# Moving the last set's output weights behind the last rows of V in a decode-attention kernel

## The chip, the cores and the metric

The kernel runs on one core of one Trainium2 chip. The metric is the device time of one execution in microseconds (us), as the median of three runs.

## The reference, cut to what matters

One token attends to two caches, A with 16 heads and B with 16 query heads on 8 key/value heads, each with 8192 positions of 256 numbers. Each result goes through an output matrix `wo`, and a gate mixes the two rows of 448 numbers.

```python
def _A_ref(x, k_cache, v_cache, wq, wo):
    ...
    scores = jnp.einsum("bhqd,bhkd->bhqk", q, k_cache) * (Dh ** -0.5)
    p = _softmax(scores, axis=-1)
    o = jnp.einsum("bhqk,bhkd->bhqd", p, v_cache)
    return (lambda x, *d: x.transpose(*d))(o, 0, 2, 1, 3).reshape(B, Sq, H * Dh) @ wo
...
g = _sigmoid((x * gate_w).sum(-1, keepdims=True))
a = _A_ref(x, A_k_cache, A_v_cache, A_wq, A_wo)
b = _B_ref(x, B_k_cache, B_v_cache, B_wq, B_wo)
return g * a + (1 - g) * b
```

## The kernel before, in words

The work is cut into eight sets. A set holds one key/value head of B with its two query heads (unit 2) and two heads of A (units 0 and 1), and the units are done in the order 2, 0, 1 (`UNITS`). Everything is 32-bit. A unit's K and V come from memory in 4 MB transfers, two per unit for K and two for V, into a ring of five slots of 4 MB (`slot`). One loop runs over the transfers: at step i it issues K of step i and V of step i-1, then computes `scores` for step i (K times the query, exponentials, a transpose into `pr`), then `attend` for step i-1 (V times `pr`, summed in PSUM in the tile `o`). All of these loads are issued by SP, in program order, into one queue that the chip's 16 DMA engines work off; an issue waits until its slot has been read and until an earlier landing has freed the semaphore it counts on.

When a unit is done, `combine` and `column` work out the softmax weights of its rows on small tiles, `take` reads `o` into `ob`, `project_o` multiplies `ob` by the column of weights (`sel`) and copies the result to `ocs`, and `emit` multiplies `ocs` by the unit's part of `wo` and adds to `Y`, which stays in PSUM for the whole kernel. A set's `wo` is four heads of [128 rows, 896 numbers], 3,584 bytes a row and head; a 128-row head has 448 KB.

The last step (i = N) has no K. Before the change SP issues there, in this order: `wo` of heads 2 and 3, `wo` of head 0, the last V in pieces of 16, 8, 4 and 4 rows (`LAST_CUT`), and `wo` of head 1, the one that the last unit needs. TensorE (PE) does `combine` and `column` of the last unit, then `emit` of units 2 and 0 of the last set, then `attend` of the last V piece by piece, then `project_o` and `emit` of unit 1. For this last unit alone, `take(last=True)` copies the two halves of `o` unscaled, and `project_o` uses four products with two half columns (`selh`) in place of two.

Of the kernel before, what the change touches and what calls it, by code (L numbers as in the profile page):

```python
# [7 lines left out]
F32 = mybir.dt.float32  # L8
BF16 = mybir.dt.bfloat16
AF = mybir.ActivationFunctionType  # L10
OP = mybir.AluOpType
# [3 lines left out]
P = 128  # L15
D = 448
DH = 256
# [7 lines left out]
NS = 8  # L25
# [8 lines left out]
WQ = (2 * KF + 1) * DH  # L34
UNITS = [2, 0, 1]
LAST_CUT = [16, 8, 4, 4]


@with_exitstack
def kernel(  # L40
# [12 lines left out]
    nc = tc.nc  # L53
    scale = DH ** -0.5
# [3 lines left out]
    small = ctx.enter_context(tc.tile_pool(name="small", bufs=2))  # L58
# [7 lines left out]
    def heads(u):  # L66
        return 2 if u[1] == 2 else 1
# [42 lines left out]
    half = const.tile([P, 2], F32, name="half")  # L110
# [26 lines left out]
    def prepare():  # L137
        clear(Y, YN)
        gp = ps_s.tile([1, 1], F32, name="sm")
        for c in range(KF + 1):  # L140
            nc.tensor.matmul(gp, xs[:, c:c + 1], gw[:, c:c + 1], start=(c == 0), stop=(c == KF))
        ge = const.tile([1, 1], F32, name="ge")
        nc.scalar.activation(ge, gp, AF.Exp, scale=-1.0)
        nc.vector.tensor_scalar(ge, ge, 1.0, None, op0=OP.add)
        nc.vector.reciprocal(gate[:, 0:1], ge)
        nc.vector.tensor_scalar(gate[:, 1:2], gate[:, 0:1], -1.0, 1.0, op0=OP.mult, op1=OP.add)

    KT, VT, ST, PR, O, GS, SEL, OB, OC = ({} for _ in range(9))

    def project(u, w):  # L150

        s, r = u
        M = heads(u)
        q = ps_s.tile([P, 2, 2], F32, name="sm")
        n = 2 * DH
        for m in range(M):
            h = m if r == 2 else r
            for e in range(2):
                for c in range(KF):
                    at = c * n + h * DH + e * P  # L160
                    nc.tensor.matmul(q[:, e, m:m + 1], w[:, at:at + P], xs[:, c:c + 1], start=(c == 0), stop=False)  # L161
                at = KF * n + e * P
                nc.tensor.matmul(q[:, e, m:m + 1], w[:, at:at + P], xs[:, KF + h:KF + h + 1], start=False, stop=True)  # L163
        qb = QB[s % 2, r]
        nc.vector.tensor_scalar(qb[:, :, 16:16 + M], q[:, :, :M], -scale, None, op0=OP.mult)  # L165
# [34 lines left out]
            nc.tensor.matmul(O[u, part][32 * g:32 * (g + 1), :], pr[:, j // 2, :2 * NG * R], vt[:, j - j0:j - j0 + 2, :],  # L200
                             start=False, stop=(tt == R // M - 1 and j >= NB - 2 * NG), skip_group_check=True)

    def take(u, t, last=False):

        M = heads(u)
        part, tt = divmod(t, R // M)
        if tt != R // M - 1:
            return
        o = O.pop((u, part))
        ob1 = small.tile([P, DH], F32, name="ob1", bufs=1)  # L210
        ob = small.tile([P, DH], F32, name="ob", bufs=3)
        if last:
            nc.scalar.activation(ob1, o[:, DH:], AF.Copy)
            nc.vector.tensor_copy(ob, o[:, :DH])
            OB[u] = [(ob, SELH[0]), (ob1, SELH[1])]
        else:
            nc.scalar.activation(ob1, o[:, DH:], AF.Copy, scale=half[:, 1:2])  # L217
            nc.vector.scalar_tensor_tensor(ob, o[:, :DH], half[:, 0:1], ob1, op0=OP.mult, op1=OP.add)  # L218
            OB.setdefault(u, []).append((ob, None))

    def gather(u):
        M = heads(u)
# [34 lines left out]
                    ew[:, m, a * (n // M):(a + 1) * (n // M)][:, None, :, None].to_broadcast([1, NG, n // M, 2]),  # L257
                    rz[:, m:m + 1], None, op0=OP.mult)

    SELH = []  # L260

    def column(u, last=False):
        M = heads(u)
        cl = ps_s.tile([P, 2, 2], F32, name="sm")
        for a in range(M):
            for m in range(M):
                nc.tensor.matmul(cl[:, a, m:m + 1], WR[M][:, m, a].rearrange("p c x k -> p (c x k)"), one,  # L267
                                 start=True, stop=True)
        SEL[u] = small.tile([P, 2, 2], F32, name="sel")
        if last:  # L270
            for k in range(2):
                SELH.append(small.tile([P, 1], F32, name=f"selh{k}"))
                nc.vector.tensor_scalar(SELH[k], cl[:, 0, :1], half[:, k:k + 1], None, op0=OP.mult)
        else:
            nc.vector.tensor_copy(SEL[u][:, :M, :M], cl[:, :M, :M])

    def project_o(u):
        M = heads(u)
        oc = ps_s.tile([P, 2, 2], F32, name="sm")
        terms = [(ob, sel if sel is not None else SEL[u][:, a, :M]) for a, (ob, sel) in enumerate(OB[u])]  # L280
        for e in range(2):
            for k, (ob, sel) in enumerate(terms):
                nc.tensor.matmul(oc[:, e, :M], ob[:, e::2], sel, start=(k == 0), stop=(k == len(terms) - 1))  # L283
        ocs = small.tile([P, 2, 2], F32, name="ocs", bufs=4)
        nc.vector.tensor_copy(ocs[:, :, :M], oc[:, :, :M])  # L285
        OC[u] = ocs

    def emit(u, wt, last=False):
        for m in range(heads(u)):
            h = u[1] + m  # L290
            for e in range(2):
                for g in range(NG):
                    nc.tensor.matmul(Y[32 * g:32 * g + 1, :], OC[u][:, e, m:m + 1],  # L293
                                     wt[:, h, e, g * YN:(g + 1) * YN], start=False,
                                     stop=(last and m == heads(u) - 1 and e == 1), skip_group_check=True)


    work = [((s, r), t) for s in range(NS) for r in UNITS for t in range(0, NT, TL)]
    N = len(work)
    PER = len(UNITS) * NT // TL  # L300
    W, WO = {}, {}

    def load_wq(s):
        w = const.tile([P, 2 * WQ], F32, name="wq", bufs=1)
        nc.sync.dma_start(w, wq[s])
        for pair in range(2):
            W[s, pair] = w[:, pair * WQ:(pair + 1) * WQ]

    def load_k(i):
        u, t = work[i]  # L310
        kt = slot([TL, 2, NG, NB * BLK])
        nc.sync.dma_start(kt, of(u, a_k, b_k)[t // TL])
        KT[i] = kt
# [5 lines left out]
    def load_v(i, j0, n):  # L319
        vt = slot([n, DH])  # L320
        nc.sync.dma_start(vt, v_src(i)[:, j0:j0 + n, :])
        for k in range(0, n, ROWS):
            VT.setdefault(i, []).append((j0 + k, min(n, ROWS), vt[:, k:min(n, k + ROWS)]))

    def load_wo(s, parts):
        if s not in WO:
            WO[s] = const.tile([P, 4, 2, D], F32, name="wo", bufs=1)
        for h0, h1 in parts:
            nc.sync.dma_start(WO[s][:, h0:h1], wo[s][:, h0:h1])
# [3 lines left out]
    for i in range(N + 1):  # L333
        s = i // PER
        if i == 0:
            load_wq(0)
        if i < N:
            load_k(i)
        if i % PER == 2 and s + 1 < NS:
            load_wq(s + 1)  # L340
        if 0 < i < N:
            load_v(i - 1, 0, TL * ROWS)
        if i % PER == 0 and 0 < i < N:
            load_wo(s - 1, [(0, 4)])
        if i == N:
            load_wo(NS - 1, [(2, 4), (0, 1)])
            j0 = 0
            for n in LAST_CUT:
                load_v(N - 1, j0, n)
                j0 += n  # L350
            load_wo(NS - 1, [(1, 2)])


        if i == 0:
            for r in UNITS:
                project((0, r), W[0, 1 if r == 2 else 0])
            prepare()
        if i < N:
            u, t = work[i]
            kt = KT.pop(i)  # L360
            for k in range(TL):
                scores(u, t + k, kt[:, k])
            if t + TL == NT:
                gather(u)
                if i < N - 1:
                    COMB[i + 1] = u
        if i in COMB:
            combine(COMB[i])
        if i == N:
            u = work[N - 1][0]  # L370
            combine(u)
            column(u, last=True)
            emit((u[0], 2), WO[u[0]])
            emit((u[0], 0), WO[u[0]])
        if i > 0:
            u, t = work[i - 1]
            for j0, n, vt in VT.pop(i - 1):
                k, j = divmod(j0, ROWS)
                attend(u, t + k, j, n, vt)
                if j + n == ROWS:  # L380
                    take(u, t + k, last=(i == N))
        if i in COMB:
            column(COMB[i])
        if i - 1 in COMB:
            u = COMB[i - 1]
            project_o(u)
            if u[1] == UNITS[-1]:
                for r in UNITS:
                    emit((u[0], r), WO[u[0]])
        if s + 1 < NS and i % PER in (3, 4, 5):  # L390
            r = UNITS[i % PER - 3]
            project((s + 1, r), W[s + 1, 1 if r == 2 else 0])
    s = NS - 1
    project_o((s, 1))
    emit((s, 1), WO[s], last=True)

    ys = const.tile([P, YN], F32, name="ys")
    nc.vector.tensor_copy(ys, Y)
# [59 lines left out]
```

## Time and profile before

| | |
|---|---|
| median of 3 runs | 1021.46 us (1021.17 to 1021.71) |
| the profiled execution | 1021.16 us, its span in the profile 1019.3 us |
| PE busy | 660.9 us (65% of the span) |
| DVE busy, ACT busy | 209.2 us (21%), 98.9 us (10%) |
| moved by DMA | 432.68 MB, mean 425 GB/s |

The span runs from the first to the last recorded instruction; the execution's own time is 1.9 us longer. Times in the profile's views count from the span's start. PEld is PE's weight load, which overlaps its matmuls. A 32-bit matmul appears as two records, so `x28` is 14 matmuls. A share of DMA is the mean over 16 engines: 0.50 can be eight busy engines.

### The profile page before, as it was taken

To read this page: it belongs to the slowest core of one execution; us is meant where nothing else is said; L and a number is where in the kernel's file an instruction comes from. 1 tells how busy PE (TensorE), PEld (TensorE's weight loads), DVE (VectorE), ACT (ScalarE), POOL (GpSimd) and SP (SyncE) were. 2 spreads that over 40 slices of the span, in tenths; PEclk is the share of its full clock that TensorE was granted. 3 is DMA by queue.
4 is the path that set the end of the run, shared out by engine and by line. 5 is a ranking of instruction groups with operands and counts; after the bars stand their busy time and mean duration, and the time that the engine had idled before them with its cause. 6 is when DMAs were issued, how large, how long until landed. Compare 5 with 4: busy or idle time off the path is not lost.

```text
span 1019.3 us, 10424 instructions
## 1 busy us (share of the span) xinstructions
PE 660.9 (65%) x4493; PEld 250.1 (25%) x4493; DVE 209.2 (21%) x650; ACT 98.9 (10%) x258; POOL 0.6 (0%) x6
## 2 busy tenths in 40 slices
PE   6666757477575765749656487455875557746765
PEld 5113212133121321214212133121421214212212
DVE  1222212212122121222112221222212222121221
ACT  0101001000011000110001000010001100001000
POOL 0000000000000000000000000000000000000000
PEclk9768867786677887777667776787867878777668
DMA  9999999999999999999999999999999999999995
GB/s 394 424 430 431 430 436 427 431 430 432 429 431 431 428 431 430 432 430 430 428 430 429 431 430 431 432 426 431 431 430 434 429 430 428 429 432 431 431 426 241
DMA packets 17189, 432.68 MB, mean 425 GB/s; under 512 B 2168, under 2 KB 2168, under 8 KB 2808
## 3 DMA queue, kind: packets, MB, share of 16 engines
q1 hardware_dynamic: 16856, 432.02, 98.8%
q8 instruction: 35, 0.57, 0.2%
q14 instruction: 10, 0.08, 0.0%
q10 hardware_dynamic: 288, 0.00, 0.0%
HBM read 432.02 MB, written 0.00 MB: 424 GB/s over the span
## 4 chain that ended last, share of the span: by engine, by line
DMA 79%; PE 15%; another core or an unknown queue 4%; DVE 1%; issue 0%; ACT 0%; DVEq 0%; ACTq 0%
DMA slot<-in_a_v_dram 32%; DMA slot<-in_a_k_dram 32%; DMA slot<-in_b_k_dram 9%; PE sc L176 7%; PE o L200 6%; DMA slot<-in_b_v_dram 5%; PE sm L161 1%; DMA wq<-in_wq_dram 1%; PE sm L267 0%; PE sm L163 0%; DVE pr L187 0%; ACT ew L246 0%; PE o L133 0%; PE sm L283 0%
## 5 line engine op out<-in xcount | busy, mean ns | idle before, releaser
L200 PE MATMUL o<-slot,pr 128*32 128x512 f32 x1536 | 263.5, 846 | 205.3 <-DMA slot<-in_a_v_dram 112.4
L176 PE MATMUL sc<-slot,qb 128*32 128x512 f32 x1536 | 270.4, 868 | 127.2 <-DMA slot<-in_b_k_dram 65.9
L200 PEld LDWEIGHTS o<-slot,pr 128*32 128x32 f32 x1536 | 59.9, 147 | 372.6 <-issue 159.8
L187 DVE STREAM_TRANSPOSE pr<-px 128x512 f32<-128x512 f32 x96 | 68.4, 713 | 363.6 <-PE o L200 318.2
L176 PEld LDWEIGHTS sc<-slot,qb 128*32 128x32 f32 x1536 | 69.8, 151 | 287.0 <-issue 284.6
L184 ACT ACTIVATE px<-sc,st 128x512 f32<-128x512 f32 x96 | 66.0, 688 | 626.5 <-DVE st L182 626.5
L180 DVE TENSOR_REDUCE mn<-sc 128x1 f32<-128x512 f32 x96 | 65.3, 680 | 289.1 <-PE sc L176 286.5
L161 PE MATMUL sm<-xs,wq 128*128 128x1 f32 x384 | 60.5, 273 | 8.5 <-DMA wq<-in_wq_dram 8.5
L161 PEld LDWEIGHTS sm<-xs,wq 128*128 128x128 f32 x384 | 57.1, 223 | 8.6 <-issue 8.5
L163 PE MATMUL sm<-xs,wq 128*128 128x1 f32 x128 | 26.2, 274 | 0.0
L246 ACT ACTIVATE ew<-sm,mnr 1x16 f32<-1x16 f32 x32 | 7.6, 261 | 177.3 <-DVE mnr L244 177.3
L163 PEld LDWEIGHTS sm<-xs,wq 128*128 128x128 f32 x128 | 23.1, 225 | 0.0
L267 PE MATMUL sm<-one,wr 1*128 1x1 f32 x96 | 14.3, 247 | 13.2 <-DVE wr L255 13.1
L217 ACT ACTIVATE ob<-o,half 128x256 f32<-128x256 f32 x31 | 14.7, 474 | 82.0 <-PE o L200 82.0
L283 PEld LDWEIGHTS sm<-sel,ob 128*128 128x128 f32 x124 | 16.4, 196 | 21.7 <-issue 20.0
L267 PEld LDWEIGHTS sm<-one,wr 1*128 1x128 f32 x96 | 12.7, 184 | 35.0 <-issue 17.4
L218 DVE SCALAR_TENSOR_TENSOR ob<-o,half,ob 128x256 f32<-128x256 f32 x31 | 14.9, 481 | 21.7 <-ACT ob L217 21.3
L184 ACT ACTIVATION_READ_ACCUMULATOR px<-sc,st 128x1 f32 x96 | 18.5, 193 | 0.0
L283 PE MATMUL sm<-sel,ob 128*128 128x2 f32 (+1 forms) x124 | 18.3, 261 | 0.0
L165 DVE TENSOR_SCALAR qb<-sm 128x2 f32<-128x2 f32 (+1 forms) x24 | 3.9, 162 | 66.2 <-PE sm L163 66.2
L182 DVE TENSOR_TENSOR st<-mn,cap 128x1 f32<-128x1 f32 x96 | 15.3, 160 | 3.3
L293 PE MATMUL Y<-wo,ocs 128*1 128x112 f32 x512 | 13.9, 259 | 0.3 <-DVE ocs L285 0.3
(48 smaller groups left out, 95.5 us busy)
## 6 DMA issues: line engine op xcount, KB each, us to landing
slot<-in_a_k_dram SPq DMA_DIRECT2D x32, 4096.0 KB, 47.0
slot<-in_a_v_dram SPq DMA_DIRECT2D x31, 4096.0 KB, 44.4
slot<-in_b_k_dram SPq DMA_DIRECT2D x16, 4096.0 KB, 45.6
slot<-in_b_v_dram SPq DMA_DIRECT2D x16, 4096.0 KB, 47.6
wq<-in_wq_dram SPq DMA_DIRECT2D x8, 1792.0 KB, 48.9
wo<-in_wo_dram SPq DMA_DIRECT2D x7, 1792.0 KB, 47.0
slot<-in_a_v_dram SPq DMA_DIRECT2D x1, 2048.0 KB, 41.2
slot<-in_a_v_dram SPq DMA_DIRECT2D x1, 1024.0 KB, 33.7
```

Source lines behind the costliest of these rows:

```text
L161: nc.tensor.matmul(q[:, e, m:m + 1], w[:, at:at + P], xs[:, c:c + 1], start=(c == 0), stop=False)
L163: nc.tensor.matmul(q[:, e, m:m + 1], w[:, at:at + P], xs[:, KF + h:KF + h + 1], start=False, stop=True)
L176: nc.tensor.matmul(sc[32 * g:32 * (g + 1), :], qb[:, e, at:at + 32], kt[:, e, g, :], start=(e == 0), stop=(e == 1), skip_group_check=True)
L180: nc.vector.tensor_reduce(mn, sc, axis=AX.X, op=OP.min)
L182: nc.vector.tensor_tensor(st[:, 0, t:t + 1], mn, CAP[M][:, tt:tt + 1], op=OP.min)
L184: nc.scalar.activation(px, sc, AF.Exp, bias=st[:, 0, t:t + 1], scale=-1.0, accum_out=st[:, 1, t:t + 1])
L187: nc.vector.transpose(pr.rearrange("p (q r k) -> p q k r", r=BLK, k=2), px.rearrange("p (q k c) -> p q k c", c=BLK, k=2))
L200: nc.tensor.matmul(O[u, part][32 * g:32 * (g + 1), :], pr[:, j // 2, :2 * NG * R], vt[:, j - j0:j - j0 + 2, :], start=False, stop=(tt == R ...
L217: nc.scalar.activation(ob1, o[:, DH:], AF.Copy, scale=half[:, 1:2])
L218: nc.vector.scalar_tensor_tensor(ob, o[:, :DH], half[:, 0:1], ob1, op0=OP.mult, op1=OP.add)
L267: nc.tensor.matmul(cl[:, a, m:m + 1], WR[M][:, m, a].rearrange("p c x k -> p (c x k)"), one, start=True, stop=True)
L283: nc.tensor.matmul(oc[:, e, :M], ob[:, e::2], sel, start=(k == 0), stop=(k == len(terms) - 1))
```

## The change

Nothing changes ahead of the last step, except that `wo` now holds B's two heads first and A's two behind them in memory, so that unit 2 uses heads 0 and 1, unit 0 head 2 and unit 1 head 3 (`HEAD_AT`). In the last step all V pieces are issued first. Then comes head 3 of `wo`, the last unit's, cut by rows into DMAs of 94, 32 and 2 (94 is 2 x 47; by the change's title most of this part goes to two DMA engines), then heads 0, 1 and 2. PE does none of the output products ahead of the last `attend`; they follow in the order unit 2 first head, (project_o), unit 2 second head, unit 1, unit 0. The special form of `take`, `column` and `project_o` for the last unit is gone, and this unit is treated like the others.

```diff
+HEAD_AT = {2: 0, 0: 2, 1: 3}
+LAST_ROWS = [94, 32, 2]
...
-    def take(u, t, last=False):
+    def take(u, t):
...
-        if last:
-            nc.scalar.activation(ob1, o[:, DH:], AF.Copy)
-            nc.vector.tensor_copy(ob, o[:, :DH])
-            OB[u] = [(ob, SELH[0]), (ob1, SELH[1])]
-        else:
-            nc.scalar.activation(ob1, o[:, DH:], AF.Copy, scale=half[:, 1:2])
-            nc.vector.scalar_tensor_tensor(ob, o[:, :DH], half[:, 0:1], ob1, op0=OP.mult, op1=OP.add)
-            OB.setdefault(u, []).append((ob, None))
+        nc.scalar.activation(ob1, o[:, DH:], AF.Copy, scale=half[:, 1:2])
+        nc.vector.scalar_tensor_tensor(ob, o[:, :DH], half[:, 0:1], ob1, op0=OP.mult, op1=OP.add)
+        OB.setdefault(u, []).append(ob)
...
         if i == N:
-            load_wo(NS - 1, [(2, 4), (0, 1)])
             j0 = 0
             for n in LAST_CUT:
                 load_v(N - 1, j0, n)
                 j0 += n
-            load_wo(NS - 1, [(1, 2)])
+            load_wo(NS - 1, [])
+            p0 = 0
+            for n in LAST_ROWS:
+                nc.sync.dma_start(WO[NS - 1][p0:p0 + n, 3:4], wo[NS - 1][p0:p0 + n, 3:4])
+                p0 += n
+            load_wo(NS - 1, [(0, 1), (1, 2), (2, 3)])
...
-            column(u, last=True)
-            emit((u[0], 2), WO[u[0]])
-            emit((u[0], 0), WO[u[0]])
+            column(u)
...
     s = NS - 1
+    emit((s, 2), WO[s], [0])
     project_o((s, 1))
-    emit((s, 1), WO[s], last=True)
+    emit((s, 2), WO[s], [1])
+    emit((s, 1), WO[s])
+    emit((s, 0), WO[s], last=True)
...
-        "wo": _np.concatenate([wo(get("A_wo")), wo(get("B_wo"))], axis=2),
+        "wo": _np.concatenate([wo(get("B_wo")), wo(get("A_wo"))], axis=2),
```

On SP, the end of the program before (partitions x numbers per partition; in brackets the semaphores that an issue waits for, `DMAHW` for landings of earlier DMAs):

```order
L321 DMA slot<-in_a_v_dram 128x8192 [waits DMAHW2_49,PE_49]
L329 DMA wo<-in_wo_dram 128x1792
L329 DMA wo<-in_wo_dram 128x896
L321 DMA slot<-in_a_v_dram 128x4096 [waits DMAHW3_49,PE_49]
L321 DMA slot<-in_a_v_dram 128x2048 [waits DMAHW4_49,PE_49]
L321 DMA slot<-in_a_v_dram 128x1024 [waits DMAHW5_49,PE_49]
L321 DMA slot<-in_a_v_dram 128x1024 [waits DMAHW6_49,PE_49]
L329 DMA wo<-in_wo_dram 128x896
L399 DMA out_dram<-ys 4x112 [waits DMAHW7_49,DVE_49]
```

The same place on SP after the change:

```order
L310 DMA slot<-in_a_v_dram 128x8192 [waits DMAHW2_49,PE_49]
L310 DMA slot<-in_a_v_dram 128x4096 [waits DMAHW3_49,PE_49]
L310 DMA slot<-in_a_v_dram 128x2048 [waits DMAHW4_49,PE_49]
L310 DMA slot<-in_a_v_dram 128x1024 [waits DMAHW5_49,PE_49]
L310 DMA slot<-in_a_v_dram 128x1024 [waits DMAHW6_49,PE_49]
L342 DMA wo<-in_wo_dram 94x896
L342 DMA wo<-in_wo_dram 32x896
L342 DMA wo<-in_wo_dram 2x896
L318 DMA wo<-in_wo_dram 128x896 [waits DMAHW7_49]
L318 DMA wo<-in_wo_dram 128x896 [waits DMAHW0_49]
L318 DMA wo<-in_wo_dram 128x896 [waits DMAHW1_49]
L393 DMA out_dram<-ys 4x112 [waits DMAHW2_49,DVE_49]
```

Two `wo` DMAs left the place ahead of the last V, and the last three `wo` DMAs now wait at their issue: for the landing of the last whole V transfer, of the 16-row piece and of the 8-row piece.

On PE, the end of the program before, from the last unit's `combine` on (`pos` and `wr` are operands of `combine` and `column`, `o<-slot,pr` is `attend`, `sm<-sel,ob` is `project_o`, `Y<-wo,ocs` is `emit`):

```order
L237 MATMUL sm<-pos,gs 1x16 x2
L267 MATMUL sm<-one,wr_104 128x1
L293 MATMUL Y<-wo,ocs 1x112 x24
L200 MATMUL o<-slot,pr 32x512 x16
L283 MATMUL sm<-selh_4166,ob 128x1
L283 MATMUL sm<-selh_4168,ob_4210 128x1
L283 MATMUL sm<-selh_4166,ob 128x1
L283 MATMUL sm<-selh_4168,ob_4210 128x1
L293 MATMUL Y<-wo,ocs 1x112 x8
```

The same place on PE after the change:

```order
L234 MATMUL sm<-pos,gs 1x16 x2
L262 MATMUL sm<-one,wr_104 128x1
L202 MATMUL o<-slot,pr 32x512 x16
L282 MATMUL Y<-wo,ocs 1x112 x8
L272 MATMUL sm<-sel,ob 128x1 x2
L282 MATMUL Y<-wo,ocs 1x112 x24
```

The 24 products that stood ahead of the last `attend` are behind it, eight of them ahead of `project_o`, and two of the four products of `project_o` are gone.

The same end of PE's program after the change, from the last `attend` matmul on, with its waits (`DMAHW7` is here the landing of head 0 of `wo`, `DMAHW0` of head 1, `DMAHW4` to `6` of head 3's three parts, `DMAHW1` of head 2):

```order
L202 MATMUL o<-slot,pr 32x512
L282 MATMUL Y<-wo,ocs 1x112 [waits DMAHW7_49]
L282 MATMUL Y<-wo,ocs 1x112 x7
L272 MATMUL sm<-sel,ob 128x1 [waits DVE_49]
L272 MATMUL sm<-sel,ob 128x1
L282 MATMUL Y<-wo,ocs 1x112 [waits DMAHW0_49]
L282 MATMUL Y<-wo,ocs 1x112 x7
L282 MATMUL Y<-wo,ocs 1x112 [waits DMAHW5_49,DMAHW6_49,DMAHW4_49,DVE_49]
L282 MATMUL Y<-wo,ocs 1x112 x7
L282 MATMUL Y<-wo,ocs 1x112 [waits DMAHW1_49]
L282 MATMUL Y<-wo,ocs 1x112 x7
```

The products with unit 0's part, for which the last DMA brings the weights, now stand last.

## Rows read from the trace of the kernel before

**Rows 1.** The page: DMA busy tenths and GB/s in forty slices.

```profile
DMA  9999999999999999999999999999999999999995
GB/s 394 424 430 431 430 436 427 431 430 432 429 431 431 428 431 430 432 430 430 428 430 429 431 430 431 432 426 431 431 430 434 429 430 428 429 432 431 431 426 241
```

**Rows 2.** The chain that ended last, from 994 us: start us, us, what.

```profile
994.67 17.76 DMA slot<-in_a_v_dram
...
1012.48 1.08 PE o L200 x4
...
1013.57 0.39 ACT ob L213
...
1013.99 0.44 DVE ob L214
...
1014.47 1.12 PE sm L283 x8
...
1015.83 0.61 PE Y L293 x16
...
1016.46 0.28 DVE ys L398
```

**Rows 3.** Timeline of PE from 1004 us: start us, us, then the group.

```profile
1004.46 0.63 PE L283 MATMUL sm<-sel,ob 128*128 128x1 f32 x4
...
1007.02 0.35 PE L267 MATMUL sm<-one,wr 1*128 1x1 f32 x2 [1.76 <-DVE wr L255]
1007.30 1.33 PE L293 MATMUL Y<-wo,ocs 128*1 128x112 f32 x48
1008.45 3.74 PE L200 MATMUL o<-slot,pr 128*32 128x512 f32 x28
```

**Rows 4.** Timeline of PE's weight loads (PEld) in the last attends.

```profile
1008.88 0.13 PEld L200 LDWEIGHTS o<-slot,pr 128*32 128x32 f32 x4 [0.30 <-issue]
1009.31 0.13 PEld L200 LDWEIGHTS o<-slot,pr 128*32 128x32 f32 x4 [0.30 <-issue]
1009.88 0.13 PEld L200 LDWEIGHTS o<-slot,pr 128*32 128x32 f32 x4 [0.43 <-DMA slot<-in_a_v_dram]
...
1011.14 0.14 PEld L200 LDWEIGHTS o<-slot,pr 128*32 128x32 f32 x4 [0.84 <-DMA slot<-in_a_v_dram]
```

**Rows 5.** Windows: busy us by engine; last three: PE clock, DMA share, GB/s.

```profile
990.00:995.00 5.00, 4.94 (x33) 1.20 (x25) 1.07 (x3) 0.78 (x2) 0.00 (x0) 0.75 1.01 426
1004.00:1005.00 1.00, 1.00 (x12) 0.55 (x4) 0.00 (x0) 0.00 (x0) 0.00 (x0) 1.00 0.88 362
1006.00:1007.00 1.00, 0.00 (x0) 0.01 (x1) 0.77 (x4) 0.00 (x0) 0.00 (x0) 1.00 0.58 239
1009.50:1010.00 0.50, 0.50 (x8) 0.12 (x4) 0.00 (x0) 0.00 (x0) 0.00 (x0) 1.00 0.52 209
1011.00:1011.50 0.50, 0.50 (x6) 0.14 (x4) 0.00 (x0) 0.00 (x0) 0.00 (x0) 1.00 0.32 127
1012.50:1013.00 0.50, 0.50 (x4) 0.12 (x4) 0.00 (x0) 0.00 (x0) 0.00 (x0) 1.00 0.10 36
1018.00:1018.50 0.50, 0.00 (x0) 0.00 (x0) 0.00 (x0) 0.00 (x0) 0.00 (x0) 0.50 0.02 4
```

**Rows 6.** The page: DMA queue, kind: packets, MB, share of 16 engines.

```profile
q8 instruction: 35, 0.57, 0.2%
```

**Rows 7.** Timeline of SP's queue (SPq): its last DMA issues.

```profile
966.14 28.86 SPq L321 DMA_DIRECT2D slot<-in_a_v_dram  x4
995.05 0.42 SPq L329 DMA_DIRECT2D wo<-in_wo_dram  x1
1016.76 0.65 SPq L399 DMA_DIRECT2D out_dram<-ys  x1
```

**Rows 8.** Timeline of ACT and DVE: the previous unit's output read.

```profile
986.37 0.47 ACT L217 ACTIVATE ob<-o,half 128x256 f32<-128x256 f32 x1 [1.76 <-PE o L200]
...
986.88 0.48 DVE L218 SCALAR_TENSOR_TENSOR ob<-o,half,ob 128x256 f32<-128x256 f32 x1 [1.16 <-ACT ob L217]
```

More of the change, by code (lines that the diff above doesn't have):

```diff
@@ L258, in combine, with column @@
                     rz[:, m:m + 1], None, op0=OP.mult)
-    SELH = []
-    def column(u, last=False):
+    def column(u):
         M = heads(u)
@@ L269, in column @@
         SEL[u] = small.tile([P, 2, 2], F32, name="sel")
[L270 to L275, printed above, removed]
+        nc.vector.tensor_copy(SEL[u][:, :M, :M], cl[:, :M, :M])
     def project_o(u):
@@ L279, in project_o @@
         oc = ps_s.tile([P, 2, 2], F32, name="sm")
-        terms = [(ob, sel if sel is not None else SEL[u][:, a, :M]) for a, (ob, sel) in enumerate(OB[u])]
         for e in range(2):
-            for k, (ob, sel) in enumerate(terms):
-                nc.tensor.matmul(oc[:, e, :M], ob[:, e::2], sel, start=(k == 0), stop=(k == len(terms) - 1))
+            for a, ob in enumerate(OB[u]):
+                nc.tensor.matmul(oc[:, e, :M], ob[:, e::2], SEL[u][:, a, :M], start=(a == 0), stop=(a == M - 1))
         ocs = small.tile([P, 2, 2], F32, name="ocs", bufs=4)
@@ L286, in project_o, with emit @@
         OC[u] = ocs
-    def emit(u, wt, last=False):
-        for m in range(heads(u)):
-            h = u[1] + m
+    def emit(u, wt, ms=None, last=False):
+        for m in range(heads(u)) if ms is None else ms:
+            h = HEAD_AT[u[1]] + m
             for e in range(2):
@@ L294, in emit @@
                                      wt[:, h, e, g * YN:(g + 1) * YN], start=False,
-                                     stop=(last and m == heads(u) - 1 and e == 1), skip_group_check=True)
+                                     stop=(last and e == 1), skip_group_check=True)
     work = [((s, r), t) for s in range(NS) for r in UNITS for t in range(0, NT, TL)]
@@ L380 @@
                 if j + n == ROWS:
-                    take(u, t + k, last=(i == N))
+                    take(u, t + k)
         if i in COMB:
```

## Prediction

> **What bounds the kernel now.** The page's slices come first: the DMA engines are busy from the start to the last slice, at about 430 GB/s [rows 1]. So until the last loads land the time is bytes over bandwidth; the change moves the same bytes and touches nothing before the last step. What is left to move is the tail.
>
> The chain of waits comes second. Its last DMA link is the last 4-row V piece, landing at 994.67 + 17.76 = 1012.43 [rows 2]. Behind it stand the last four attend records on PE, ACT's and DVE's reads of `o`, the eight records of project_o, the copy, 16 emit records and the copy of `Y` from 1016.46. These 4.03 us are bare: nothing runs beside them.
>
> Third, the timeline of PE before that landing. `column` ends at 1007.37, the 48 emit records of units 2 and 0 run from 1007.30, and attend begins only at 1008.45 [rows 3]. With data there a group of four attend records takes 0.43 us (1008.88 to 1009.31); later groups are released by V at 1009.88 and 1011.14, the last at 1012.48 [rows 2, 4]. So V sets the pace there, at about 1.3 us for a 512 KB piece where PE needs 0.43.
>
> Fourth, the windows of the DMA share. It is full at 990 to 995 us, but 0.88 at 1004, 0.58 at 1006, 0.52 at 1009.5, 0.32 at 1011 and 0.10 at 1012.5 [rows 5]. Times 16 that is 9.3 engines still busy at 1006, 8.3 at 1009.5, 5 at 1011: about seven engines have finished by 1006.5, one ends near 1009.5, eight end between 1010.5 and 1013. A likely part of the unevenness is the instruction fetch, 35 packets with 0.2% of 16 engines' span [rows 6]: 0.002 x 16 x 1019.3 = 33 us; spread over eight engines it makes 4 us on each.
>
> **The change, part by part.**
>
> *V earlier.* Three heads of `wo` leave the queue ahead of the V pieces. Of a 128-row head each engine moves 8 rows if they are spread evenly, so 24 rows of 3,584 bytes. At 426 GB/s over 16 engines [rows 5] one moves 26.6 GB/s, a row takes 0.135 us, and 24 rows 3.2 us. The 8-row piece should land at 1006.7 in place of 1009.9, the two 4-row pieces at 1007.9 and 1009.2. The 16-row piece, which made no wait at 1008.45 [rows 3], should be there by 1005.2 at the latest.
>
> *PE starts earlier.* With the 48 emit records gone from in front, attend starts at 1007.38, behind `column` (ends 1007.02 + 0.35). Eight groups at 0.43 put the last group's start at 1007.38 + 7 x 0.43 = 1010.39. By then the last V piece has been there 1.2 us, so PE itself paces the attend, and of the 3.2 us gained by V only 1012.48 - 1010.39 = 2.09 us arrive. [...]
>
> *The reads of `o`.* The general form takes 0.47 us on ACT and 0.48 on DVE [rows 8], where the chain has 0.39 and 0.44 [rows 2]: +0.12 us.
>
> *project_o.* Four records in 0.63 us [rows 3] in place of eight in 1.10 to 1.12 [rows 2]: -0.47 (the two half columns that DVE no longer makes lay off the path and are worth nothing).
>
> *emit.* 48 records take 1.33 us [rows 3], 16 take 0.56 to 0.61 [rows 2]; each more costs (1.33 - 0.56)/32 = 0.024. The first eight products run while ACT and DVE read `o`, the second eight beside the copy to `ocs`; both cost nothing there, and without that cover 16 x 0.024 = 0.38 us each. On the path stand 32 records in place of 16: +0.38.
>
> *SP's new waits.* The three full-height `wo` issues wait for the last whole V, the 16-row and the 8-row piece. Behind them SP has only the output, so only `wo` can be late. The last issue leaves at about 1006.7. The output DMA, issued at 1016.76 [rows 7], shows its first packets in the window from 1018.0 [rows 5], so 1.3 us later: 1008, while the slowest engines still have V until 1009.2. No engine that ends the queue runs dry. If the delay were 5 us, 1011.7 plus 1.1 us for 8 rows is still before PE wants it.
>
> *When PE wants `wo`.* Head 0 from about 1010.8, and it delays project_o only if it lands after 1012.0; the last head from 1016.46 - 2.05 - 0.63 = about 1013.8. If all rows of head 3 are spread evenly, the end stays at 1013.0 [rows 5], in time. If 94 of them go to two engines, those two have 47 + 2 + 1 + 24 = 74 rows, the others 26, against 32 before: +5.7 us on two, -0.8 us on fourteen. This cost is zero for two engines that end before 1013.8 - 5.7 = 1008.1 now, and up to 1013.0 + 5.7 + 0.6 - 1016.4 = +2.9 us for the last ones. No row says which two they are. I take zero, the value of the seven early engines and of an even spread.
>
> [...]
>
> *Sum.* -2.09 + 0.12 - 0.47 + 0.38 = -2.06 us. Against the profiled execution's own 1021.16 (span 1019.3 and 1.9 around it) that is 1019.1. This execution lies 0.3 us under the median of 1021.46, so I predict 1019.4.
>
> **The rivals.**
>
> *The middle engine.* One of the two is the engine that ends near 1009.6: its last row lands at 1015.3, emit of unit 0 ends 0.61 later at 1015.9, against 1016.44: -0.5 us, 1020.9. For it: the one-engine step between 0.58 and 0.52. Against it: one engine of sixteen.
>
> *The late engines.* One of the two is among the eight that end from 1010.5 to 1013.0: `wo` lands at 1016.2 to 1018.7, `Y` is done at 1016.8 to 1019.3, and the time is 1021.9 to 1024.3. PE would stand in front of a product with unit 2's or unit 0's weights while all else is done. It decides from an end of 1010.1 now (no gain left), and passes 0.2% of loss from 1012.2. For it: half of the engines are of this kind. [...]
>
> [...]
>
> *V is not earlier.* If landings hung on the issue (the pieces are issued from 966 to 995 [rows 7]) and not on the queue, the last V would still land at 1012.4, and what is left is +0.12 - 0.47 + 0.38, about 0: 1021.5. Against it: pieces land 1.3 us apart [rows 2, 4], the pace of 32 KB an engine at 26.6 GB/s, so the queue sets them.
>
> **How the numbers follow.** Forecast 0.5, the middle engine 0.2, V not earlier 0.05, late engines 0.25. The first holds from 1019.0 to 1019.7 by itself (steps of the sum read to about 0.1 us, medians to 0.3). Up to 1022.3 lie the middle engine, V not earlier and the near half of the late engines, together 0.87 of the chance; what lies above, about 0.12, is left out. As the forecast could also be some tenths better, the range is 1018.8 to 1022.3. A difference of 0.2%, 2.04 us, is about what a measurement tells from no change, and the forecast lies on that edge (1019.42): a little over half of its chance counts as faster, 0.32; slower is the late engines' far half, 0.13; the rest, 0.55, is the same.
>
> **What the changed profile would show.** Attend's last 32 records in one run from about 1007.4, with weight loads 0.43 us apart and no wait for V; the last V landing near 1009.2; project_o as four records near 1012.4; `Y` copied near 1014.4. In the windows the DMA share should fall to two engines' 0.12 at some time after 1008. If PE waits for `wo` in the last products, the late or middle engines are the answer, and the length of that wait says which. A clock below 1.00 in the attend, or a V wait there, would break the second step of the sum.

## The result, and the profile after

The changed kernel took 1023.57 us, the kernel before 1021.44 us on the same chip: 2.13 us more, a ratio of 1.0022 [1.0015, 1.0029]. The forecast was 1019.4 us in a range up to 1022.3, so the time lies above the range. With the same kernel but head 3 of `wo` loaded in one piece, in place of 94, 32 and 2 rows, the time is 1019.12 us (2.24 us under the kernel before on its chip). The rest of the change does about what was forecast, and the cut by rows costs about 4.4 us. All times of kernels are medians, and leave out one execution of e2 (2651 us) and one of g4 (1070 us) that ran in a slow state.

The profiled execution took 1023.45 us, its span is 1021.7 us. First the chain of waits of the changed kernel (start us, us, what):

```profile
999.04 16.29 DMA wo<-in_wo_dram
...
1015.37 0.56 PE Y L282 x16
1015.93 0.56 PE sm L272 x4
...
1016.51 2.10 PE Y L282 x48
...
1018.62 0.28 DVE ys L392
```

Where the chain of before ran through the last V piece, the attend, the reads of `o` and project_o [rows 2], none of these but project_o is left. The end now hangs on one `wo` load, head 0, which lands at 999.04 + 16.29 = 1015.33. Its first user is the first output product. `Y` is copied at 1018.62, where before had 1016.46 [rows 2]: +2.16 us, the whole of the loss.

The timeline of SP's issues, PE and its weight loads (start us, busy us, engine, line, operation, count; in brackets the idle time before it and what ended it):

```profile
1004.74 3.79 SPq L318 DMA_DIRECT2D wo<-in_wo_dram  x2
...
1007.39 5.71 PE L202 MATMUL o<-slot,pr 128*32 128x512 f32 x32
...
1012.04 0.14 PEld L202 LDWEIGHTS o<-slot,pr 128*32 128x32 f32 x4 [0.51 <-DMA slot<-in_a_v_dram]
...
1015.37 0.30 PEld L282 LDWEIGHTS Y<-wo,ocs 128*1 128x1 f32 x16 [3.19 <-DMA wo<-in_wo_dram]
...
1016.51 2.05 PE L282 MATMUL Y<-wo,ocs 128*1 128x112 f32 x48
1017.63 0.48 PEld L282 LDWEIGHTS Y<-wo,ocs 128*1 128x1 f32 x16 [0.43 <-DMA wo<-in_wo_dram]
```

The attend starts at 1007.39, as forecast. But the last V piece lets PE go on only at 1012.04, less than half a us earlier than before [rows 2], where 3.2 us earlier was forecast. After that PE stands 3.19 us in front of a product for `wo`. Meanwhile `o` is read out (ACT at 1013.14, 0.47 us; DVE at 1013.64, 0.48 us, the forecast sizes) and waits from 1014.12.

Why both loads are late shows in the windows of the changed kernel (busy us of PE, PEld, DVE, ACT and POOL; the last three columns are PE's clock, the DMA share, where a little over 1 is full, and GB/s):

```profile
1000.00:1002.00 2.00, 2.00 (x16) 0.52 (x12) 0.09 (x1) 0.00 (x0) 0.00 (x0) 0.51 1.02 351
1002.00:1004.00 2.00, 2.00 (x16) 0.44 (x8) 0.83 (x3) 0.00 (x0) 0.00 (x0) 0.63 0.76 251
1004.00:1005.00 1.00, 1.00 (x12) 0.65 (x8) 0.00 (x0) 0.00 (x0) 0.00 (x0) 1.00 0.61 201
1005.00:1006.00 1.00, 0.15 (x4) 0.03 (x2) 0.61 (x4) 0.26 (x1) 0.00 (x0) 1.00 0.95 247
1006.00:1008.00 2.00, 1.09 (x6) 0.70 (x10) 0.81 (x5) 0.00 (x0) 0.00 (x0) 0.72 0.91 227
1008.00:1010.00 2.00, 2.00 (x16) 0.44 (x12) 0.00 (x0) 0.00 (x0) 0.00 (x0) 0.50 0.84 221
1010.00:1012.00 2.00, 2.00 (x20) 0.49 (x12) 0.00 (x0) 0.00 (x0) 0.00 (x0) 0.93 0.93 245
1012.00:1014.00 2.00, 1.09 (x8) 0.14 (x4) 0.35 (x1) 0.47 (x1) 0.00 (x0) 1.00 0.53 176
```

Before moved 239 GB/s at 1006 us with a share of 0.58 [rows 5], so 239 / (0.58 x 16) = 25.8 GB/s for each busy engine. The changed kernel moves 227 with a share of 0.91: 15.6 GB/s for each. Already at 1000 us the share is full and the rate 351, not the 426 of [rows 5]. At 1006 to 1012 nearly all engines are busy, and slow, at once. The kept trace also has the duration of every DMA packet, which no view prints: a 4,096-byte packet of the last V pieces takes 0.162 us in the kernel before, and 0.225 us in the mean (up to 0.47) in the changed kernel at 1000 to 1010 us.

Between 1002 and 1005 the share itself is low. Here SP's new waits show: head 0 of `wo` was issued at 999.04, but heads 1 and 2 only at 1004.74 and 1008.20, when the 16-row and the 8-row piece of V had landed. The share falls to 0.61 and is back at 0.95 after the issue of 1004.74. So some engines had no work for a while, because V was slow.

### The profile page after: what moved, and what is told of

It reads as the page before. It is cut to its first block, busy times and chain, and to the rows that moved or that the text cites. A ratio compares the mean times of both kernels' runs of the same rounds, so it can differ in the third digit from the quotient of the medians.

```text
span 1021.7 us, 10419 instructions
## 1 busy us (share of the span) xinstructions
PE 645.2 (63%) x4489; PEld 252.2 (25%) x4489; DVE 207.8 (20%) x649; ACT 98.8 (10%) x258; POOL 0.6 (0%) x6
## 2 busy tenths in 40 slices
DMA packets 17337, 432.68 MB, mean 424 GB/s; under 512 B 2188, under 2 KB 2188, under 8 KB 2956
## 4 chain that ended last, share of the span: by engine, by line
DMA 79%; PE 17%; another core or an unknown queue 3%; DVE 1%; issue 0%; ACT 0%; DVEq 0%; ACTq 0%
DMA slot<-in_a_v_dram 39%; DMA slot<-in_a_k_dram 27%; DMA slot<-in_b_k_dram 10%; PE sc L178 7%; PE o L202 6%; PE sm L163 2%; DMA wo<-in_wo_dram 2%; DMA xs<-in_x_dram 1%; PE sm L165 1%; PE sm L262 0%; PE Y L282 0%; PE sm L272 0%; DVE pr L189 0%; ACT ew L243 0%
## 5 line engine op out<-in xcount | busy, mean ns | idle before, releaser
L202 PE MATMUL o<-slot,pr 128*32 128x512 f32 x1536 | 251.6, 813 | 208.5 <-DMA slot<-in_a_v_dram 114.9
L178 PE MATMUL sc<-slot,qb 128*32 128x512 f32 x1536 | 259.1, 836 | 137.0 <-DMA slot<-in_b_k_dram 69.3
L178 PEld LDWEIGHTS sc<-slot,qb 128*32 128x32 f32 x1536 | 67.1, 146 | 290.0 <-issue 289.5
L163 PE MATMUL sm<-xs,wq 128*128 128x1 f32 x384 | 65.2, 285 | 8.3 <-DMA xs<-in_x_dram 8.3
L163 PEld LDWEIGHTS sm<-xs,wq 128*128 128x128 f32 x384 | 61.9, 239 | 8.4 <-DMA xs<-in_x_dram 8.3
L165 PE MATMUL sm<-xs,wq 128*128 128x1 f32 x128 | 28.5, 292 | 0.0
L165 PEld LDWEIGHTS sm<-xs,wq 128*128 128x128 f32 x128 | 25.7, 249 | 0.0
L272 PE MATMUL sm<-sel,ob 128*128 128x1 f32 (+1 forms) x128 | 19.0, 261 | 0.0
```

The costliest lines, as they stand in the source:

```text
L178: nc.tensor.matmul(sc[32 * g:32 * (g + 1), :], qb[:, e, at:at + 32], kt[:, e, g, :], start=(e == 0), stop=(e == 1), skip_group_check=True)
L272: nc.tensor.matmul(oc[:, e, :M], ob[:, e::2], SEL[u][:, a, :M], start=(a == 0), stop=(a == M - 1))
```

## The experiments

Ratios are to the kernel before, run on the same chip, with a 95% interval.

The expectations name theories by letters. A: a load cut by rows slows the transfers of all engines. B: only the two engines that carry 74 rows are late, and they set the end. C: V and `wo` disturb each other in their new order, with or without the cut. After the first four runs A was split: A1, it lies in how rows are dealt to engines; A2, in where the rows lie in memory. After the next four A1 was split: P, it matters which rows of on-chip memory an engine writes beside the others; Q, any load of other than 128 rows is slow.

### The parts of the change: e1_whole, e2_cut96, e3_cutonly, e4_products

**e1_whole** is the changed kernel with head 3 in one DMA.

```diff
-LAST_ROWS = [94, 32, 2]
+LAST_ROWS = [128]
```

> The changed kernel, but with head 3 of wo as one DMA of 128 rows in place of 94, 32 and 2. Theory A (the 94-row DMA on two engines slows the transfers of all engines while it runs): with the cut gone the last V piece lands at about 1009.2 us and the weight waits on PE go, the busy DMA engines keep 26 GB/s each to the end, and the time is 1019.0 to 1020.0 us. Theory B (the two engines are simply late ones and carry 74 rows in place of 32): the same 1019 to 1020 us, but with the slow packets not tied to the cut. Theory C (V and wo disturb each other whenever wo stands behind V): no gain, 1022.5 to 1024 us.

Measured: 1019.12 us, 0.9982 [0.9973, 0.9991]. It beats both kernels, and C falls: the order by itself disturbs nothing. With two DMAs fewer, SP also waits less here: the three `wo` heads are issued at 996.83, 997.29 and 998.96, so the price of the cut includes the late issues that it causes in the changed kernel. Its windows, with the columns of those above:

```profile
1000.00:1002.00 2.00, 2.00 (x16) 0.44 (x12) 0.00 (x0) 0.00 (x0) 0.00 (x0) 0.50 0.99 409
1006.00:1008.00 2.00, 1.34 (x14) 0.71 (x18) 0.63 (x3) 0.00 (x0) 0.00 (x0) 1.00 0.61 242
1010.00:1012.00 2.00, 1.35 (x27) 0.58 (x19) 0.48 (x1) 0.47 (x1) 0.00 (x0) 1.00 0.38 139
```

The share falls as in before [rows 5], at 242 / (0.61 x 16) = 24.8 GB/s for each busy engine. Its timeline of PE and PEld:

```profile
1006.93 3.64 PE L202 MATMUL o<-slot,pr 128*32 128x512 f32 x32
1009.54 0.13 PEld L202 LDWEIGHTS o<-slot,pr 128*32 128x32 f32 x4 [0.30 <-issue]
1011.22 0.30 PEld L282 LDWEIGHTS Y<-wo,ocs 128*1 128x1 f32 x16 [1.55 <-DMA wo<-in_wo_dram]
1013.44 0.30 PEld L282 LDWEIGHTS Y<-wo,ocs 128*1 128x1 f32 x16 [0.44 <-DMA wo<-in_wo_dram]
```

The attend runs without a V wait to its last group at 1009.54, so the last V piece is there by then, at least 2.9 us earlier than before [rows 2], when no load is cut by rows. Head 0 releases PE at 1011.22, 4.15 us earlier than with the cut. The last records of `Y` wait for the last `wo`, which lands at 1013.4.

**e2_cut96** cuts head 3 into 96 and 32 rows.

```diff
-LAST_ROWS = [94, 32, 2]
+LAST_ROWS = [96, 32]
```

> Head 3 in DMAs of 96 and 32 rows, sizes that sixteen engines divide. Theory A in the form that two engines alone do it: like one DMA of 128 rows, 1019 to 1020 us. Theory A in the form that any cut which deals rows otherwise than 8 to an engine does it: the DMA share stays high at a low GB/s behind the V pieces, and the time is 1021 to 1024 us. Theory B: 1019 to 1020 us.

Measured: 1021.52 us, 1.0002 [0.9993, 1.0011], 2.4 us above e1, as the second form of A has it. 96 and 32 rows lose about half of what 94, 32 and 2 lose. One window of its trace:

```profile
1000.00:1002.00 2.00, 2.00 (x16) 0.50 (x12) 0.39 (x1) 0.00 (x0) 0.00 (x0) 0.58 1.08 312
```

At a full share it moves 312 GB/s: every engine is busy, and together they bring three quarters of the 426 of [rows 5]. Two late engines alone (B) can't make that.

**e3_cutonly** is the kernel before, with only its last DMA, head 1 behind the V pieces, cut by rows.

```diff
-            load_wo(NS - 1, [(1, 2)])
+            p0 = 0
+            for n in LAST_ROWS:
+                nc.sync.dma_start(WO[NS - 1][p0:p0 + n, 1:2], wo[NS - 1][p0:p0 + n, 1:2])
+                p0 += n
```

> The kernel before, with its order of loads and products, but its last wo DMA (head 1 there) cut into 94, 32 and 2 rows. Theory A: the early engines reach the 94 rows at about 1004 us, the late engines' V pieces are slowed from there on, the last V lands at 1014 to 1017 us in place of 1012.4, and the time is 1023 to 1027 us. Theory B with late engines: V lands at 1012.4 as before, the two engines end at 1016 to 1018.5 us with their rows, and the time is 1022 to 1024 us, with no slow packets of others. If the two engines are early and nothing is slowed: 1021.4 us.

Measured: 1022.63 us, 1.0010 [1.0002, 1.0019], so 1.27 us lost. In its timeline the last group of the attend waits for V:

```profile
1013.92 0.14 PEld L201 LDWEIGHTS o<-slot,pr 128*32 128x32 f32 x4 [1.16 <-DMA slot<-in_a_v_dram]
```

That is 1.4 us later than the last group of before [rows 2], though the cut load stands behind V in the queue. A load cut by rows delays transfers that were queued ahead of it. The time lies in B's range and under A's; the late V is A's sign, at a smaller size than A had.

**e4_products** is the changed kernel with its loads in the order of before (diff against the changed kernel).

```diff
+            load_wo(NS - 1, [(0, 2), (2, 3)])
             j0 = 0
             for n in LAST_CUT:
                 load_v(N - 1, j0, n)
                 j0 += n
-            load_wo(NS - 1, [])
-            p0 = 0
-            for n in LAST_ROWS:
-                nc.sync.dma_start(WO[NS - 1][p0:p0 + n, 3:4], wo[NS - 1][p0:p0 + n, 3:4])
-                p0 += n
-            load_wo(NS - 1, [(0, 1), (1, 2), (2, 3)])
+            load_wo(NS - 1, [(3, 4)])
```

> The loads of before in their old places in the queue (two heads, one head, V, one head), but the products, the general read of o and project_o of the changed kernel. All theories: V lands at 1012.4 as before, and behind it the chain differs by +0.12 - 0.47 + 0.38 us, so 1021.0 to 1022.0 us. If PE's part of the change costs more than reckoned, it shows here: 1022 us or more.

Measured: 1020.96 us, 0.9996 [0.9987, 1.0004]: about 0.4 us, not told from nothing. Without earlier V the order of the products brings next to nothing.

### Where the cut's price comes from: f1 to f4

**f1_source** is the changed kernel, with head 3's numbers a second time in memory in an array of their own, so that a row's source lies next to the next row's.

```diff
-                nc.sync.dma_start(WO[NS - 1][p0:p0 + n, 3:4], wo[NS - 1][p0:p0 + n, 3:4])
+                nc.sync.dma_start(WO[NS - 1][p0:p0 + n, 3:4], wo_end[p0:p0 + n, :])
```

> The changed kernel with its cut of 94, 32 and 2 rows, but the rows of head 3 are read from a small array of their own in which they lie one behind the other (in the changed kernel a row of 3,584 bytes every 14,336). Theory A1 (where the cut's rows are read does not matter, the slowing comes from dealing them to other engines than usual): as the changed kernel, 1022.5 to 1024.5 us, DMA share high at 200 to 280 GB/s. Theory A2 (engines reading the same strided array out of step disturb each other in memory): 1019 to 1020.5 us and 26 GB/s for each busy engine.

Measured: 1024.55 us, 1.003 [1.002, 1.004], no better than the changed kernel. Where the rows lie in memory is not the cause: A2 falls.

**f2_steady96** and **f4_steady64** cut the `wo` loads of the seven earlier sets in the kernel before, in mid-run: 96 and 32 rows, or 64 and 64. **f3_steadycols** is the control: as many DMAs for the same bytes, but cut by heads, all with 128 rows.

```diff
-            load_wo(s - 1, [(0, 4)])
+            load_wo(s - 1, [])
+            p0 = 0
+            for n in [96, 32]:
+                nc.sync.dma_start(WO[s - 1][p0:p0 + n], wo[s - 1][p0:p0 + n])
+                p0 += n
```

In f4 the list is `[64, 64]`. In f3 the one changed line is:

```diff
-            load_wo(s - 1, [(0, 4)])
+            load_wo(s - 1, [(0, 3), (3, 4)])
```

> The kernel before with the wo loads of sets 0 to 6 (1,792 KB each, in the middle of the stream) cut into 96 and 32 rows; the last set as before. Theory A1: each of the seven loads slows all engines while any of them is in it; an engine needs 4.3 us for it and engines stand up to 7 us apart, so some 4 to 11 us at 1.2 to 1.7 times the duration: 1 to 5 us a load, 1028 to 1055 us. If the slowing belongs to the tail alone, where engines run dry: 1021 to 1022 us.

> The kernel before with the same seven loads cut into two DMAs of 128 rows each, three heads and one head. Control for the number of DMAs and for the semaphores that the issues wait for. Theory A1: 1021 to 1022 us. If more DMAs by themselves cost time: above 1023 us.

> The kernel before with the same seven loads cut into 64 and 64 rows, 4 rows to an engine in each. Theory A1 (rows dealt to other engines than usual): slower than the control, by about as much as the cut at 96 or up to half of it if some rows still meet their usual engine. If only sizes other than powers of two hurt: 1021 to 1022 us.

Measured: f2 1085.11 us, 1.0599 [1.0573, 1.0625]; f4 1085.86 us, 1.061 [1.0583, 1.0638]; f3 1021.82 us, 1.0004 [0.9995, 1.0012]. Against the control, a load cut by rows costs (1085.11 - 1021.82) / 7 = 9.0 us in f2 and 9.1 in f4, nearly twice the most that A1 had reckoned (5 us). Single executions spread from 1077 to 1091 us, so f2 and f4 are not told apart. The whole load is 1.84 MB, 4.3 us at 430 GB/s. So it is not the tail and not the number of DMAs. The page of f2 (busy tenths, GB/s, packets):

```profile
DMA  9999999999999999999999999999999999999992
GB/s 394 432 425 436 428 336 430 432 427 402 356 429 429 431 372 375 429 432 428 345 396 430 429 433 311 387 429 432 433 309 378 431 433 430 308 366 429 431 421 112
DMA packets 17301, 432.68 MB, mean 397 GB/s; under 512 B 2280, under 2 KB 2280, under 8 KB 2920
```

And that of f3:

```profile
DMA packets 18197, 432.68 MB, mean 424 GB/s; under 512 B 2280, under 2 KB 2280, under 8 KB 3816
```

The seven dents in GB/s are the seven loads, and the busy row above shows nothing of them: no engine is left idle, so the work doesn't lie on two. f3 has more packets, and more small ones, and loses nothing.

### Which rows: g1_mid64, g2_low64, g4_high64

What is left is which rows of on-chip memory a DMA writes. Here sets 1 to 6 load only 64 of the 128 rows of their `wo`, in one DMA; the other rows keep set 0's numbers, in one buffer for all sets. So half of six sets' weights is left out, the same half of the bytes in each of the three kernels, which differ in the range of rows alone, on chip and in memory.

```diff
-            load_wo(s - 1, [(0, 4)])
+            load_wo(s - 1, [(0, 4)] if s == 1 else [])
+            if s > 1:
+                nc.sync.dma_start(WO[s - 1][32:96], wo[s - 1][32:96])
```

In g2 the range is `[0:64]`, in g4 `[64:128]`.

> The kernel before, but of the wo loads of sets 1 to 6 only rows 32 to 95 are loaded (half of these six sets' weights is left out; the other rows keep set 0's). 5.5 MB less is 12.9 us less at 426 GB/s. Theory P (what counts is which rows of on-chip memory an engine writes: in a 128-row load the engine of a row is the usual one, and two engines on the rows of one share its path; dealt four by four, rows 32 to 95 fall one engine to a path): the full gain, 1007 to 1010 us. Theory Q (any load of other than 128 rows is slow): as rows 0 to 63, 15 us and more above that.

> The same six half loads, but rows 0 to 63. Theory P (dealt four by four, all sixteen engines fall on the paths of eight): each load takes twice as long or more and slows what runs beside it; the two cuts of 64 cost 9 us a set, so one costs 4 to 5 us: 1008.5 + 6 x 4.5 = 1030 to 1040 us. Theory Q: the same 1030 to 1040 us for all three.

> The same six half loads, but rows 64 to 127. Theory P: like rows 0 to 63, since all engines fall on the paths of the other eight: 1030 to 1040 us. If only the low rows are slow: 1007 to 1010 us.

Measured: g1 1008.91 us, 0.9875 [0.986, 0.989]; g2 1051.35 us, 1.0311 [1.0252, 1.0371]; g4 1050.95 us, 1.0314 [1.0264, 1.0364]. Six halves of 0.92 MB left out are worth 6 x 2.13 = 12.8 us at 430 GB/s, and g1 gains 12.7: rows 32 to 95 cost what their bytes cost, and Q falls. Rows 0 to 63 cost (1051.35 - 1008.91) / 6 = 7.1 us more for each load, rows 64 to 127 cost 7.0, as P has it, though at a higher price than expected. (Their executions spread over 10 to 15 us, so it is about 7 for both.) The rows also differ at the source; but f2 reads the same rows as f3 and is slow, so the source rows by themselves are not the cause. DMA issues on the page of g1 (KB each, median us from issue to landing; one of the seven is the last set's load of two whole heads):

```profile
DMA packets 16805, 427.18 MB, mean 424 GB/s; under 512 B 2168, under 2 KB 2168, under 8 KB 2808
wo<-in_wo_dram SPq DMA_DIRECT2D x7, 896.0 KB, 44.8
```

The same on the page of g2:

```profile
DMA packets 16805, 427.18 MB, mean 408 GB/s; under 512 B 2168, under 2 KB 2168, under 8 KB 2808
wo<-in_wo_dram SPq DMA_DIRECT2D x7, 896.0 KB, 51.4
```

Packets, bytes and packet sizes are the same to the last. Windows of g2 around one such load:

```profile
515.00:520.00 5.00, 4.39 (x24) 1.30 (x28) 0.69 (x1) 0.00 (x0) 0.00 (x0) 0.50 1.07 419
520.00:525.00 5.00, 1.80 (x20) 0.43 (x12) 1.69 (x5) 1.56 (x4) 0.00 (x0) 0.84 0.98 228
525.00:530.00 5.00, 0.14 (x4) 0.15 (x8) 0.00 (x0) 0.00 (x0) 0.00 (x0) 0.50 1.09 249
```

The window of g1 in which its load of the same set runs:

```profile
509.00:514.00 5.00, 1.85 (x20) 0.58 (x12) 1.97 (x5) 1.56 (x4) 0.00 (x0) 0.96 0.99 417
```

In g2 all engines are busy for ten us at a little over half the rate. At 430 GB/s the load itself is 2.1 us, so the K and V transfers beside it are slowed as well. The packet records of the two traces show this directly. In g1 a K or V packet of 32,768 bytes takes 1.22 us and a packet of 14,336 bytes, a row of these loads (and of `wq`), 0.54 us (medians). In g2 326 packets of the first size and 361 of the second take over one and a half times as long, 2.3 and 1.1 us in the mean; in g1 only 5 and 17 do. Divided by sixteen engines, g2's K and V packets take 25.1 us longer than g1's, and those of the load's size 12.3 us. That is 6.2 us a load of the 6.6 by which the two profiled executions differ, and two thirds of it fall on transfers that write all 128 rows.

### The other half of the change: g3_loads

**g3_loads** is e1 with the products of units 2 and 0 ahead of the attend, as before (diff against e1).

```diff
             column(u)
+            emit((u[0], 2), WO[u[0]])
+            emit((u[0], 0), WO[u[0]])
...
-    emit((s, 2), WO[s], [0])
     project_o((s, 1))
-    emit((s, 2), WO[s], [1])
-    emit((s, 1), WO[s])
-    emit((s, 0), WO[s], last=True)
+    emit((s, 1), WO[s], last=True)
```

> The loads alone: V first and wo behind it in whole heads, but the products in the order of before (units 2 and 0 ahead of the last attend). All theories: PE stands before attend until the last head lands at about 1013.4, then 0.8 us of products, 4.1 us of attend, 0.95 for the reads of o, 0.85 for project_o and its copy, 0.6 for the last products: Y done at 1020.7 in place of 1016.4, 1025 to 1026.5 us.

Measured: 1025.64 us, 1.0039 [1.0024, 1.0053], 4.0 us lost. From its chain of waits:

```profile
999.09 14.44 DMA wo<-in_wo_dram
...
1013.57 0.93 PE Y L282 x16
1014.49 5.14 PE o L202 x32
```

The attend stands behind products whose weights land at 1013.5. Part of the loss is PE's pace: these 16 records of products took 0.93 us, where e1's last 16 took 0.61 at a clock of 1.00, and the attend took 5.14 us in place of the 4.1 reckoned (this execution took 1026.89 us). That a lower clock made both longer is an estimate from these numbers. The loads alone lose 4.0 us, the products alone gain at most 0.4, both together gain 2.24 (e1).

## Why the prediction was wrong, step by step

**What bounds the kernel, and the early steps: right.** Until about 1000 us both kernels are full at about the same rate (at 995 to 1000 us before moves 403 GB/s at a share of 0.96, the changed kernel 401 at 0.95). In e1 the attend starts at 1006.93 (forecast 1007.38), each group takes the forecast 0.43 us, no V wait breaks it, project_o runs at 1011.72 (forecast near 1012.4), and `Y` is copied at 1014.07 (forecast near 1014.4). The sum was -2.06 us; e1 measures -2.24. Its end is set by the last `wo` at 1013.40, close to the 1013.0 that the prediction gave for an even spread. The total fits in part by luck: the attend began 0.45 us earlier than forecast, and the end then stood for the last `wo`, a wait that the sum did not have.

**The step that failed** is the price of the cut: "This cost is zero for two engines that end before 1013.8 - 5.7 = 1008.1 now, and up to 1013.0 + 5.7 + 0.6 - 1016.4 = +2.9 us for the last ones." The prediction took zero. It counted rows for each engine at 0.135 us a row, worked out from a rate at which only 128-row loads run, and held the pace of the other engines fixed. The runs showed that a row's time isn't fixed while a load cut by rows is under way: 15.6 GB/s for each busy engine in place of 25 to 26, for V and the whole heads too. A 3,584-byte packet, one row of a head, takes 0.20 us in the mean from 1000 us on, where it takes 0.15 in before. So "V earlier" fell with it, from 3.2 us to 0.4. Measured, the cut costs about 4.4 us, and both ends of the bound were too low. Between the profiled executions of e1 and the changed kernel the copy of `Y` moves by 4.55 us: 4.15 us are head 0's landing (1015.33 for 1011.18), and 0.4 what stands behind it (3.25 us from the first product to the copy, for 2.85 in e1). Both signs that the prediction named for a broken second step showed: a V wait in the attend (0.51 us, to 1012.04), and a clock below 1.00 (0.50 at 1008 to 1010).

A second term, put at nothing, failed with it: "No engine that ends the queue runs dry." It had V on time. In the changed kernel V was late, SP's last two `wo` issues waited for it, and the share fell to 0.61 at 1004 to 1005. What these waits cost by themselves no run shows.

**The rivals.** The late engines' rival named the time (1021.9 to 1024.3) and the place (PE in front of a product for `wo`), but by another mechanism, so its time is luck. Its mechanism would have left fourteen engines done early and the DMA share falling to 0.12; the share was 0.93 at 1010 to 1012 and 0.53 at 1012 to 1014. In e2 and f2 the loss is there with all engines busy (e2: a share of 1.08 at 312 GB/s at 1000 to 1002; f2: 1.06 at 247 GB/s at 540 to 545). That two engines carry the 94 rows, on which this rival's 74 rows rest, no view says, but the pages count for it: of packets under 512 B before has 2168 and f2 and f3, with seven DMAs more, 2280: 16 for each. The changed kernel has three DMAs more, the parts of head 3, and 2188: 20 for the three. Sixteen for the 32 rows and two each for the 94 and the 2 make 20, if each engine of a DMA adds one (an estimate). That these two engines add something of their own is possible: the changed kernel is about 2 us above e2. So is a part for the late issues: e2 issued heads 1 and 2 at 999.02 and 1005.28, the changed kernel at 1004.74 and 1008.20. No view names the engine of a packet, so which two they are, and what each adds, stays open. "V not earlier" came nearly true, by slow engines and not by the issues.

**What is shown, and what is argued.** Shown: at equal bytes, packets and sizes, rows 32 to 95 load at full pace, and rows 0 to 63 or 64 to 127 do not (g1, g2, g4); neither the layout at the source (f1) nor, in mid-run, the number of DMAs (f3) matters. Argued: that two engines then write into the same part of on-chip memory. No run shows which engine writes which rows, nor the paths of P's expectations; these are the author's picture, and what the runs show is the order of g1, g2 and g4. Why 96 + 32 rows cost as much as 64 + 64 (9.0 and 9.1 us a load) no run shows either.

A doubled time for the load alone, from which P's expectation starts, would be 2.1 us more a load (an estimate: 0.92 MB at 430 GB/s); the runs measure about 7. The packets of g2 fit both numbers: the load's own take 12.3 / 6 = 2.05 us longer for each load, and K's and V's take 25.1 / 6 = 4.2.

## What to carry to other kernels

Cut a load by columns, not by rows: as long as every DMA writes all 128 rows, the cut was free here (f3, a ratio of 1.0004), while 96 + 32 or 64 + 64 rows cost 9 us a load, on transfers all around it. The sign is a full DMA share at a low GB/s (0.98 at 228 in g2); read the two columns together, since the share alone looks healthy. And weights that are needed last belong behind the last data only together with products in the order of landing: the products alone brought -0.4 us, not told from nothing, the loads alone +4.0, and both -2.24.

## What was not expected of the hardware

The price of a load with shared rows is several times its own time (about 7 us for 2.1 us of bytes in g2), most of it in other transfers (25.1 of 37.4 us), of which 326 packets take 2.3 us for 1.22, and it reaches transfers that were queued ahead of it (in e3 the last group of the attend waits for V until 1013.92, 1.4 us later than before).

PE's clock: in the changed kernel it falls to 0.50 at 1007 to 1010 us, after PE had stood 1.76 us ahead of the last record of `column`. The attend took 5.71 us, mostly for it, where e1 took 3.64 at 1.00 after the same 1.76 us. Behind this idle stretch the clock stayed at 1.00 in before [rows 5], e1 and f1 (1.00 at 1006 to 1010), but not here, nor in e2 and e3 (0.50 at 1008 to 1010). In those three the clock had also risen later (0.57 to 0.63 at 1002 to 1004, for 0.81 to 0.97 in the others). In e4 it was 1.00 already at 1000 to 1002 and fell all the same (0.50 at 1008 to 1010), after PE had stood 1.76 us and then 1.71 us for V. On the end it had little effect, since `o` was read by 1014.12 and `wo` came at 1015.33. Why it falls in the one and not in the other was not tried.
